# One order for five engines: an earlier bias chain, zeros for a waiting TensorE, a third operand set, one branch at the end

## The chip, the cores and the metric

The kernel runs on one core of one Trainium2 chip. The metric is the device time of one execution in microseconds (us). The engines are TensorE (PE for matmuls, PEld for its weight loads), VectorE (DVE), ScalarE (ACT), GpSimd (POOL) and SyncE (SP), which issues most DMAs.

## The reference

Three layers follow each other, all in float32 (the weights of the second layer are float64).

```python
# 1: causal attention with decay, q, k, v: (4, 8, 576, 64), f: (4, 8, 576)
scores = q @ k.T / sqrt(64)
cum = cumsum(log(clip(f, 1e-4, 1.0)), axis=-1)
scores = where(causal, -1e9, scores + cum[..., :, None] - cum[..., None, :])
attn = exp(scores - max(scores)); attn = attn / (sum(attn) + 1e-9)
x = (attn @ v), heads side by side        # (2304, 512)
# 2: dense layer with ELU, w_in (512, 2048), w_out (2048, 512)
h = x @ w_in; g = where(h > 0, h, exp(min(h, 0)) - 1); x = g @ w_out
# 3: eight experts, each token goes to one
logits = x @ w_gate + modality_bias[modality_id]; e = argmax(logits)
out = softmax(logits)[e] * (relu(x @ w1[e]) @ w2[e])
```

## The kernel before, in words

Every float32 product is made from two halves of an operand, a rounded one and its remainder, so TensorE multiplies two or three times for each product.

**Attention** (`attn`, `pair`) works on 16 pairs of heads, numbers 0 to 15. For a pair, SP loads q and k (`loads`, tiles `rq` and `rk` of pool `rqk`), TensorE transposes them (L572), ScalarE writes the rounded halves into `kb` and `qm` (L582), VectorE the remainders into `kx` and `qx` (L587), and SP copies the rounded halves beside the remainders (L593, L595). A first product `s1` (L617, with a causal mask from L620) gives the row maxima (VectorE, L635 and L637); these are transposed (L656) and written into row 96 of `qm` (L659). The second product `s2` (L670 and L673) then yields the scores transposed and already less their maximum, ScalarE takes the exponential (L692), GpSimd cuts the diagonal blocks (L697). The row sums come either from TensorE (pairs in `PE_SUM`) or from additions on GpSimd or VectorE (L705, chosen by `ADDPOOL`).

**The bias chain** (`attn_prep`) makes the decay term: SP loads f (L437), VectorE clips it (L443), ScalarE takes the logarithm (L446), VectorE adds it up along the row (L449), multiplies by -8 (L451), rounds (L452) and takes the remainder (L453). The two results, `nbr(0)` and `nbr(1)`, go to rows 64 and 65 of `kb`: for pair 0 by four small DMAs from SBUF (L559), for the other pairs by way of DRAM (L457, then L555). No `s1` can begin before its rows are there. `ms` fills the constant rows of `kb` and `qm` on GpSimd (L461 to L463).

The four tiles `kx`, `kb`, `qx`, `qm` are a *set*; there are two sets, and pair i takes whichever is free. Tile `xB` holds the attention's output for the second group of rows and is empty until the second batch element begins.

**Dense layer** (`convs`, `moe1`): in the first part, float64 weights are read as raw words and turned into two float32 halves in eight steps on ScalarE, VectorE and GpSimd (L849 to L879) and spilled to DRAM; `C7POOL` says whether the last step (L879) runs on VectorE or GpSimd for each of a weight block's two halves. The token rows go through in four steps (`STEPS`), each with eight groups of weights; the activation takes four operations `e1` to `e4` (L930 to L943), where `E4POOL` gives the last of a step to GpSimd. **Experts** (`route`, `tables`, `slot`): tokens are sorted into lists, `tables` makes the counts, and 2 + 9 slots of fixed size do the work; each slot ends in a scatter to the output (L1354). `rest` stands behind them: for either kind of slot it loads a count into a register of each engine (L1464) and jumps over further slots when there are none (L1465).

**The order** on all engines is written out ahead of time by a planner (`Sched`): each operation has a cost and a priority, and a simulated machine picks the lowest priority among those that could start. The table `SHIFT` moves the priorities of named groups of operations, so it decides the order on every queue, SP's included. Buffers come from named pools with a fixed number of slots.

Of the kernel before, what the change touches and what calls it, by code (L numbers as in the profile page):

```python
# [30 lines left out]
P = 128  # L31
# [169 lines left out]
class Kern:  # L201
# [71 lines left out]
    def pools(self):  # L273
# [14 lines left out]
        sc.pool("rqk", 2, tl(A, [96, 6, 2, D], F32, "rqk"))  # L288
# [16 lines left out]
    def consts(self):  # L305
# [4 lines left out]
        nc.vector.memset(self.ones64, 1.0)  # L310
        self.maskU = cp.tile([P, P], BF16, name="maskU")
# [112 lines left out]
    def attn_prep(self):  # L424
# [8 lines left out]
        def row(k):  # L433
            return sc[k][0:32, 0:S]
# [13 lines left out]
        def v2():  # L448
            nc.vector.tensor_tensor_scan(out=row(C), data0=row(O), data1=row(F), initial=0.0,  # L449
                                         op0=ALU.mult, op1=ALU.add)  # L450
            nc.vector.tensor_scalar(row(O), row(C), -8.0, None, op0=ALU.mult)  # L451
            nc.vector.tensor_copy(self.nbr(0), row(O))  # L452
            nc.vector.tensor_tensor(self.nbr(1), row(O), self.nbr(0).bitcast(F32), op=ALU.subtract)  # L453
# [17 lines left out]
        l = sc.op("SP", 0.45, l1, acq=[("pt", F)])  # L471
        n = sc.op("DVE", 0.6, one, acq=[("pt", O)])
        o = sc.op("DVE", 0.37, v1, [l])
        o = sc.op("ACT", 0.58, a1, [o])
        self.cumd = o = sc.op("DVE", 2.7, v2, [o, n], acq=[("pt", C)], rel=[C])
        self.nbd = o
        self.padd = sc.op("POOL", 0.6, pad, prio=0.5)
        self.nb8d = sc.op("SP", 0.9, l2, [o], rel=[O, F])
        self.sets, self.setd = [], []
        for s in range(2):  # L480
            st = {}
            for nm in ("kx", "kb", "qx", "qm"):
                st[nm] = ap.tile([P, 2, S], F32R, name=f"{nm}_{s}")
# [3 lines left out]
            sc.op("DVE", 0.18, lambda st=st: nc.vector.memset(st["ms"], 0.0), prio=-1.0)  # L487
            self.setd.append(sc.op("POOL", 2.6, lambda st=st: ms(st), prio=-1.0 + s))
            self.sets.append(st)

# [21 lines left out]
    def pair(self, i, t0, per, bg):  # L512
# [49 lines left out]
        got = op(None, 0.0, None, [], acq=[("set", st_)])  # L562
        ldb = [op("SP", 0.58 if i else 2.3, lb, [got, self.nbd if i == 0 else self.nb8d] + self.setd + self.first,
# [1001 lines left out]
```

## Time and profile before

| | |
|---|---|
| three timed runs | 924.23, 927.33, 928.87 us; median 927.33 |
| the profiled execution | 924.3 us, of which 922.4 us from the first to the last instruction |
| TensorE busy in the span | 860.8 us (93%), 5321 matmuls |
| VectorE, ScalarE, GpSimd busy | 704.1, 476.2, 284.2 us (76%, 52%, 31%) |
| moved by DMA | 174.39 MB, 189 GB/s |

The span's start is the zero of all times below. An engine counts as busy while it executes; branches, semaphore and register instructions and the issue of DMAs are not counted. Busy TensorE isn't TensorE at its best: matmuls overlap, and at the lower of its two clock levels the same work is busy for longer.

### The profile page before, as it was taken

Reading aid. Unit: us, or ns where it says so; the run is one execution under the profiler, and the core shown is the slowest. Engines: PE = TensorE matmul, PEld = TensorE weight load, DVE = VectorE, ACT = ScalarE, POOL = GpSimd, SP = SyncE. Lnnn points to the kernel's source line nnn. Section 1 sums busy time; section 2 is a strip of 40 time slices with the busy share of each in tenths; the row PEclk is TensorE's granted clock in tenths of the full one; section 3 lists DMA queues with packets and bytes.
Section 4 is the critical chain, followed back from the end, with each engine's and each line's share of the span. In section 5 each row is a group of like instructions: output and inputs, shape, how many; then the busy total and the mean of one; then the engine's idle time right before and its main releaser. Section 6 shows DMA issues by size and latency. Waiting matters only on the chain. (4 is left out here: it accounts for less than half of the span.)

```text
span 922.4 us, 15345 instructions
## 1 busy us (share of the span) xinstructions
PE 860.8 (93%) x5321; PEld 723.7 (78%) x5321; DVE 704.1 (76%) x1562; ACT 476.2 (52%) x923; POOL 284.2 (31%) x371
## 2 busy tenths in 40 slices
PE   4998998899999899999999999999999999999894
PEld 3776766676788788887777888898898888878783
DVE  6688799896899957769998569978797656677731
ACT  4676777676454464354463244346362545647520
POOL 4244467575101163024131010003013345344420
PEclk9999999999999999999999999999999999999998
DMA  6566788866963625458454525559154877688710
GB/s 138 146 189 197 213 224 225 241 241 229 286 254 107 156 82 140 157 150 218 131 183 151 182 92 183 188 215 390 73 152 152 273 235 238 237 267 283 255 62 28
DMA packets 111360, 174.39 MB, mean 189 GB/s; under 512 B 67150, under 2 KB 67168, under 8 KB 102695
## 3 DMA queue, kind: packets, MB, share of 16 engines
q1 hardware_dynamic: 108231, 163.54, 56.6%
q0 software_dynamic: 3040, 9.74, 2.8%
q8 instruction: 46, 0.75, 0.4%
q14 instruction: 43, 0.35, 0.1%
HBM read 136.87 MB, written 26.68 MB: 177 GB/s over the span
## 5 line engine op out<-in xcount | busy, mean ns | idle before, releaser
L926 PE MATMUL banks<-x_h,w_i 128*128 128x320 f32 (+1 forms) x768 | 208.1, 342 | 3.5 <-DVE ya L960 0.9
L953 PE MATMUL banks<-w_o,g_h 128*128 128x512 f32 x576 | 185.6, 403 | 4.9 <-DVE x_l L809 1.7
L926 PEld LDWEIGHTS banks<-x_h,w_i 128*128 128x128 f32 x768 | 135.8, 188 | 17.0 <-DVE ya L960 1.6
L697 POOL TENSOR_SCALAR_AFFINE_SELECT pt<-pt 128x128 f32<-128x128 f32 (+1 forms) x150 | 51.3, 356 | 276.2 <-ACT pt L692 274.4
L926 PE MATMUL banks<-x_l,w_i 128*128 128x320 f32 (+1 forms) x384 | 129.0, 336 | 0.0
L953 PEld LDWEIGHTS banks<-w_o,g_h 128*128 128x128 f32 x576 | 102.3, 190 | 26.3 <-DVE g_l L943 2.4
L953 PE MATMUL banks<-w_o,g_l 128*128 128x512 f32 x288 | 113.2, 393 | 0.0
L960 DVE TENSOR_TENSOR ya<-ya,banks 128x512 f32<-128x512 f32 x126 | 84.7, 681 | 24.5 <-PE banks L953 23.9
L930 ACT ACTIVATE e<-banks 128x320 f32<-128x320 f32 (+1 forms) x96 | 46.8, 488 | 89.2 <-PE banks L926 88.8
L692 ACT ACTIVATE pt<-banks 128x576 f32<-128x576 f32 (+4 forms) x160 | 60.4, 437 | 37.8 <-PE banks L673 32.3
L935 DVE SCALAR_TENSOR_TENSOR banks<-e,banks 128x320 f32<-128x320 f32 (+1 forms) x96 | 53.6, 558 | 32.1 <-ACT e L931 31.7
L1381 PE MATMUL banks<-xt_f_h,w_f 128*128 128x256 f32 x384 | 73.6, 286 | 3.8 <-DVE w_f L1312 1.8
L926 PEld LDWEIGHTS banks<-x_l,w_i 128*128 128x128 f32 x384 | 72.2, 188 | 4.9
L1056 DVE CUSTOM_DVE_ANT_0 junk<-ya,wgb 128x512 bf16<-128x512 f32 x104 | 71.4, 686 | 2.5 <-DMA wgb<-wgd 1.2
L1312 DVE TENSOR_TENSOR w_f<-wr_f,w_f 128x1024 fp32r<-128x1024 f32 x36 | 54.2, 1520 | 21.6 <-ACT w_f L1307 21.4
L1307 ACT ACTIVATE w_f<-wr_f 128x1024 fp32r<-128x1024 f32 x48 | 50.5, 1058 | 37.4 <-PE banks L1348 19.0
L1381 PEld LDWEIGHTS banks<-xt_f_h,w_f 128*128 128x128 f32 x384 | 61.5, 192 | 5.4 <-DVE w_f L1312 2.2
L939 ACT ACTIVATE g_h<-banks 128x320 fp32r<-128x320 f32 (+1 forms) x96 | 46.7, 487 | 36.2 <-DVE banks L935 35.6
L670 PE MATMUL banks<-qx,kx 128*128 128x288 f32 (+2 forms) x192 | 57.6, 316 | 7.8 <-ACT pt L692 2.3
L953 PEld LDWEIGHTS banks<-w_o,g_l 128*128 128x128 f32 x288 | 54.4, 189 | 12.2
L617 PE MATMUL banks<-kb,qm 96*128 96x288 f32 (+4 forms) x192 | 53.2, 366 | 11.2 <-DMA kb<-pt 5.7
L943 DVE TENSOR_TENSOR g_l<-banks,g_h 128x320 fp32r<-128x320 f32 (+1 forms) x96 | 52.7, 552 | 12.9 <-ACT g_h L939 12.4
(263 smaller groups left out, 1922.1 us busy)
## 6 DMA issues: line engine op xcount, KB each, us to landing
w_i<-wspi SPq DMA_DIRECT2D x24, 1024.0 KB
w_o<-wspo SPq DMA_DIRECT2D x24, 1024.0 KB
wr_f<-in_moe_w SPq DMA_DIRECT2D x48, 512.0 KB
wr_h<-in_moe_w SPq DMA_DIRECT2D x24, 512.0 KB
raw_o<-in_moe_w_out SPq DMA_DIRECT2D x16, 512.0 KB
raw_i<-in_moe_w_in SPq DMA_DIRECT2D x16, 512.0 KB
wspo<-w_o SPq DMA_DIRECT2D x8, 1024.0 KB
wspi<-w_i SPq DMA_DIRECT2D x8, 1024.0 KB
```

Source lines behind the costliest of these rows:

```text
L617: nc.tensor.matmul(ps[:, o:o + n], st["qm"][0:96, hh, q0:q0 + P], st["kb"][0:96, hh, c0:c0 + n], start=True, stop=not diag)
L670: nc.tensor.matmul(ps[:kn, o:o + n], st["kx"][:, hh, k0:k0 + kn], st["qx"][:, hh, c0:c0 + n], start=True, stop=False)
L692: nc.scalar.activation(d, src, AF.Exp, scale=0.125)
L697: nc.gpsimd.affine_select(out=pt[:kn, o:o + kn], in_=pt[:kn, o:o + kn], pattern=[[1, kn]], compare_op=ALU.is_ge, fill=0.0, base=0, channel ...
L926: nc.tensor.matmul(ph[:, :n], a, b[:, c, c0:c1], start=(c == 0 and k == 0), stop=(c == 3 and k == 2))
L935: nc.vector.scalar_tensor_tensor((e if E4POOL[s] else sc[hk])[:, :n], e[:, :n], -1.0, sc[hk][:, :n], op0=ALU.add, op1=ALU.max)
L943: eng.tensor_tensor(sc[gk][1][:, c0:c0 + n], sc[ek if E4POOL[s] else hk][:, :n], sc[gk][0][:, c0:c0 + n].bitcast(F32), op=ALU.subtract)
L953: nc.tensor.matmul(py, a[:, sl], b, start=(fc == 0 and k == 0), stop=(fc == 1 and k == 2))
L960: nc.vector.tensor_tensor(y, y, py, op=ALU.add)
L1056: nc.vector.tensor_tensor_reduce(out=self.junk, in0=sc[yk], in1=w, scale=1.0, scalar=0.0, op0=ALU.mult, op1=ALU.add, accum_out=V["dt"][:, ...
L1312: eng.tensor_tensor(w[:, :, 1, :], sc["wr", nm, m, u], w[:, :, 0, :].bitcast(F32), op=ALU.subtract)
L1381: nc.tensor.matmul(sc["ch", nm, f // 2][:, z * 256:(z + 1) * 256], a, b[:, c, :], start=(c == 0 and k == 0), stop=(c == 3 and k == 2))
```

## The change

- **Bias chain first.** The load of f gets the lowest priority of all; the bias operations hold their place (`lock=True`); the multiplication and rounding become one instruction, and the remainder another that reads the running sum directly. A one-element logarithm (`lg1`) stands at the start of ScalarE's program.
- **Zeros multiplied.** Twelve operations of four 128x128 by 128x256 bf16 products of zeros are put into TensorE's order near the start.
- **Constant rows.** `ms` is split in two: the ones of `qm` are written by VectorE for the first two sets (whole lower half, one instruction), the rows of `kb` by GpSimd in two instructions. An operation waits for the rows of its own set, no longer for those of both.
- **A third set**, laid over `xB`, serves pair 2. **Four buffers** instead of two for q and k.
- **One branch at the end.** `tables` also makes `left`, the largest surplus over the slots that always run; `rest` tests that once, and the two old tests stand inside.
- **Order made anew.** All of `SHIFT` and the planner's other numbers differ. With them go: `PE_SUM` from pairs 0 to 3 to pairs 0, 1, 3, 5; additions on VectorE for pairs 2, 8, 11, 13 and 15 (before: pair 15); the last conversion step wholly on GpSimd; `e4` of the dense layer's last step on GpSimd; two neighbours in the order of the expert slots exchanged.

```diff
-        sc.pool("rqk", 2, tl(A, [96, 6, 2, D], F32, "rqk"))
+        sc.pool("rqk", 4, tl(A, [96, 6, 2, D], F32, "rqk"))
...
+        self.zero = cp.tile([P, 256], BF16, name="zero")
+        nc.vector.memset(self.zero, 0.0)
+        self.lg1 = cp.tile([P, 1], F32, name="lg1")
+        nc.scalar.activation(self.lg1, self.ones64[:, 0:1], AF.Ln)
...
-            nc.vector.tensor_scalar(row(O), row(C), -8.0, None, op0=ALU.mult)
-            nc.vector.tensor_copy(self.nbr(0), row(O))
-            nc.vector.tensor_tensor(self.nbr(1), row(O), self.nbr(0).bitcast(F32), op=ALU.subtract)
+
+        def v3():
+            nc.vector.tensor_scalar(self.nbr(0), row(C), -8.0, None, op0=ALU.mult)
+
+        def v4():
+            nc.vector.scalar_tensor_tensor(self.nbr(1), row(C), -8.0, self.nbr(0).bitcast(F32), op0=ALU.mult, op1=ALU.subtract)
...
-        def ms(st):
-            for nm in ("kb", "qm"):
-                nc.gpsimd.memset(st[nm][64:128].bitcast(F32), 0.0)
-            nc.gpsimd.memset(st["qm"][64:66].bitcast(F32), 1.0)
-            nc.gpsimd.memset(st["kb"][96:97].bitcast(F32), 1.0)
+        def ms(st, z):
+            if z == 0:
+                (nc.vector if st["ones"] == "DVE" else nc.gpsimd).memset(st["qm"][64:128].bitcast(F32), 1.0)
+            else:
+                nc.gpsimd.memset(st["kb"][64:128].bitcast(F32), 0.0)
+                nc.gpsimd.memset(st["kb"][96:97].bitcast(F32), 1.0)
+
+        def warm(z):
+            for _ in range(4):
+                nc.tensor.matmul(sc["warm", 0][:, 0:256], self.zero[:, 0:P], self.zero, start=True, stop=True)
...
-        l = sc.op("SP", 0.45, l1, acq=[("pt", F)])
+        l = sc.op("SP", 0.62, l1, acq=[("pt", F)], prio=-400.0)
...
+        sc.grp = "warm"
+        a = sc.op(None, 0.0, None, acq=[("p", ("warm", 0))], prio=0.0)
+        for z in range(WARM):
+            sc.op("PE", 0.43, lambda z=z: warm(z), [a], rel=[("warm", 0)], prio=20.0 + 0.1 * z)
...
-        sc.op(None, 0.0, None, s2s_ + pe + aug, rel=[st_])
+        sc.op(None, 0.0, None, s2s_ + pe + aug, rel=[("xB", 2) if i == 2 else st_])
...
+            if k == "f":
+                more = sm([1], "more")
+                nc.vector.tensor_scalar(more, end[:, 7:8], float(-SF), 0.0, op0=ALU.add, op1=ALU.max)
+            else:
+                left = self.left = sm([1], "left", I32)
+                nc.vector.scalar_tensor_tensor(left, end[:, 7:8], float(-SH), more, op0=ALU.add, op1=ALU.max)
...
-        for k, n0, n in (("f", SF, NF), ("h", SH, NH)):
-            tot = nc.values_load(self.tot[k][0:1, 0:1], min_val=0, max_val=n)
-            with self.tc.If(tot > n0):
...
+        left = nc.values_load(self.left[0:1, 0:1], min_val=0, max_val=max(NF - SF, NH - SH))
+        with self.tc.If(left > 0):
+            for k, n0, n in (("f", SF, NF), ("h", SH, NH)):
+                tot = nc.values_load(self.tot[k][0:1, 0:1], min_val=0, max_val=n)
+                with self.tc.If(tot > n0):
...
-PE_SUM = [True, True, True, True, False, False, False, False, False, False, False, False, False, False, False, False]
+PE_SUM = [True, True, False, True, False, True, False, False, False, False, False, False, False, False, False, False]
...
-C7POOL = [False, True]
-E4POOL = [False, False, False, False]
-ADDPOOL = [True, False, False, True, True, True, True, True, True, True, True, True, True, True, True, False]
...
+C7POOL = [True, True]
+E4POOL = [False, False, False, True]
+ADDPOOL = [False, False, False, False, True, True, True, True, False, True, True, False, True, False, True, False]
...
+WARM = 12
```

## Rows read from the trace of the kernel before

**Rows 1.** Windows: stretch, its length, each engine's busy us, clock, DMA share, GB/s.

```profile
0.00:17.09 17.09, 4.80 (x24) 3.72 (x25) 11.56 (x17) 9.90 (x13) 10.47 (x21) 1.00 0.58 134
17.09:33.90 16.81, 15.88 (x67) 13.20 (x68) 10.26 (x16) 4.66 (x10) 1.52 (x5) 1.00 0.60 166
...
40.00:225.00 185.00, 169.56 (x1124) 131.60 (x1124) 163.22 (x283) 131.07 (x255) 102.19 (x142) 0.99 0.74 215
225.00:440.00 215.00, 208.02 (x1362) 176.16 (x1361) 171.34 (x419) 105.57 (x248) 53.72 (x109) 0.99 0.59 175
440.00:860.00 420.00, 409.13 (x2399) 351.64 (x2399) 323.31 (x805) 203.98 (x368) 103.01 (x84) 1.00 0.59 203
...
909.50:922.40 12.90, 0.00 (x0) 0.00 (x0) 0.75 (x1) 0.00 (x0) 0.98 (x1) 0.70 0.09 27
```

**Rows 2.** Timeline, first 18 us: start, duration, engine, line, operation [idle before <-releaser].

```profile
3.62 0.62 SPq L437 DMA_DIRECT2D pt<-in_f  x1
...
6.41 1.09 DVE L443 TENSOR_SCALAR pt<-pt 32x576 f32<-32x576 f32 x1 [4.24 <-DMA pt<-in_f]
6.63 1.28 ACT L446 ACT_TABLE_LOAD   x1
...
7.92 0.68 ACT L446 ACTIVATE pt<-pt 32x576 f32<-32x576 f32 x1
...
8.64 1.34 DVE L449 TENSOR_TENSOR_SCAN pt<-pt,pt 32x576 f32<-32x576 f32 x1
...
10.02 1.01 DVE L451 TENSOR_SCALAR pt<-pt 32x576 f32<-32x576 f32 x1
...
11.06 0.78 DVE L452 CAST pt<-pt 32x576 fp32r<-32x576 f32 x1
...
11.87 0.74 DVE L453 TENSOR_TENSOR pt<-pt,pt 32x576 fp32r<-32x576 f32 x1
...
14.70 2.48 SPq L559 DMA_DIRECT2D kb<-pt  x4
...
17.12 0.39 PE L617 MATMUL banks<-kb,qm 96*128 96x64 f32 x1 [4.81 <-DMA kb<-pt]
```

**Rows 3.** Timeline, TensorE's matmuls around 33 us and around 40 us.

```profile
33.02 0.44 PE L670 MATMUL banks<-qx,kx 128*128 128x288 f32 x1
...
33.26 0.44 PE L673 MATMUL banks<-qm,kb 128*128 128x288 f32 x1
...
40.18 0.29 PE L670 MATMUL banks<-qx,kx 128*128 128x288 f32 x1
...
40.31 0.29 PE L673 MATMUL banks<-qm,kb 128*128 128x288 f32 x1
```

**Rows 4.** Lines L1464, L1465, L1561: instruction, ns min/median/max, first to last start us.

```profile
L1464 POOLq TENSOR_LOAD <-toth x1: 305/305/305, 916.5 to 916.5; - x1
...
L1465 PEldq COMPARE_BRANCH  x2: 3651/4042/4432, 906.3 to 910.6; - x2
...
L1465 POOLq INC_SWDGE_SEM  x2: 917/932/948, 915.5 to 917.5; - x2
...
L1561 POOLq DRAIN  x3: 40/107/3168, 918.4 to 922.2; - x3
```

**Rows 5.** Lines L879, L865, L461 by themselves, same columns, whole span.

```profile
L879 DVE TENSOR_TENSOR w_i<-raw_i,w_i x8: 677/692/1371, 59.9 to 216.7; 128x512 fp32r<-128x512 f32 x8
L879 POOL TENSOR_TENSOR w_i<-raw_i,w_i x8: 1287/1306/1329, 70.7 to 221.3; 128x512 fp32r<-128x512 f32 x8
...
L865 DVE TENSOR_SCALAR raw_i<-raw_i x16: 386/428/1197, 57.2 to 218.8; 128x512 uint32<-128x512 uint32 x16
...
L461 POOL MEMSET kb<- x2: 1053/1056/1058, 1.8 to 6.1; 64x1152 f32 x2
```

**Rows 6.** Groups by shape: busy us, mean ns, idle before; VectorE 440 to 870, GpSimd overall.

```profile
L943 DVE TENSOR_TENSOR g_l<-banks,g_h 128x320 fp32r<-128x320 f32 x32 | 15.5, 486 | 2.3 <-ACT g_h L939 2.2
...
L705 POOL TENSOR_TENSOR acc<-acc,pt 128x320 f32<-128x320 f32 x22 | 20.9, 950 | 0.3
```

More of the change, by code (lines that the diff above doesn't have):

```diff
@@ L470, in attn_prep @@
         sc.prio, sc.grp = -1.0, "prep"
-        l = sc.op("SP", 0.45, l1, acq=[("pt", F)])
+        l = sc.op("SP", 0.62, l1, acq=[("pt", F)], prio=-400.0)
         n = sc.op("DVE", 0.6, one, acq=[("pt", O)])
[L473 to L480, printed above, removed]
+        o = sc.op("DVE", 0.37, v1, [l], lock=True)
+        o = sc.op("ACT", 0.68, a1, [o])
+        o = sc.op("DVE", 1.34, v2, [o, n], acq=[("pt", C)], lock=True)
+        n1 = sc.op("DVE", 0.37, v3, [o], lock=True)
+        n2 = sc.op("DVE", 0.69, v4, [n1], rel=[C], lock=True)
+        self.nbd = [n1, n2]
+        self.padd = sc.op("POOL", 1.0, pad, prio=0.5)
+        self.nb8d = sc.op("SP", 1.2, l2, [n1, n2], rel=[O, F])
+        self.sets, self.setd, self.gots = [], [], []
+        for s in range(3):
             st = {}
-            for nm in ("kx", "kb", "qx", "qm"):
-                st[nm] = ap.tile([P, 2, S], F32R, name=f"{nm}_{s}")
+            if s < 2:
+                for nm in ("kx", "kb", "qx", "qm"):
+                    st[nm] = ap.tile([P, 2, S], F32R, name=f"{nm}_{s}")
             st["ms"] = ap.tile([P, 260], F32, name=f"m_{s}")
@@ L486, in attn_prep, with third @@
             st["ma"] = ap.tile([P, 1], F32, name=f"ma_{s}")
-            sc.op("DVE", 0.18, lambda st=st: nc.vector.memset(st["ms"], 0.0), prio=-1.0)
-            self.setd.append(sc.op("POOL", 2.6, lambda st=st: ms(st), prio=-1.0 + s))
+            st["ones"] = "DVE" if s < 2 else "POOL"
+            def third(st=st):
+                for z, (a, b) in zip(sc["xB", 2], (("kx", "kb"), ("qx", "qm"))):
+                    v = z[:].rearrange("p c n -> p (c n)")
+                    st[a], st[b] = [v[:, S * 2 * i:S * 2 * i + 2 * S].rearrange("p (h s) -> p h s", h=2) for i in range(2)]
+            al = [sc.op(None, 0.0, third, acq=[("xB", ("xB", 2))], prio=0.0)] if s == 2 else []
+            sc.op("DVE", 0.18, lambda st=st: nc.vector.memset(st["ms"], 0.0), prio=-1.0 + 2 * s)
+            self.setd.append([sc.op(st["ones"], 1.1, lambda st=st: ms(st, 0), al, prio=-1.0 + 2 * s),
+                              sc.op("POOL", 2.1, lambda st=st: ms(st, 1), al, prio=-1.0 + 2 * s)])
             self.sets.append(st)
+        sc.grp = "warm"
+        a = sc.op(None, 0.0, None, acq=[("p", ("warm", 0))], prio=0.0)
+        for z in range(WARM):
+            sc.op("PE", 0.43, lambda z=z: warm(z), [a], rel=[("warm", 0)], prio=20.0 + 0.1 * z)
     def attn(self, b, t0, per):
@@ L561, in pair @@
         sc.prio, sc.grp = t0, f"a{i}t"
-        got = op(None, 0.0, None, [], acq=[("set", st_)])
-        ldb = [op("SP", 0.58 if i else 2.3, lb, [got, self.nbd if i == 0 else self.nb8d] + self.setd + self.first,
+        if i == 2:
+            sc.tiles[st_] = (None, 0, self.sets[2])
+        got = op(None, 0.0, None, self.gots, acq=[] if i == 2 else [("set", st_)])
+        if i < 2:
+            self.gots.append(got)
+        setd = self.setd[i] if i < 3 else []
+        ldb = [op("SP", 0.58 if i else 2.3, lb, [got] + (self.nbd if i == 0 else [self.nb8d]) + setd + self.first,
                   rel=() if i else [("pt", "f"), ("pt", "one")])]
@@ L602, in pair @@
                 v = (nm, hh, key)
-                his[nm, hh] = op("ACT", 0.14 + S / 1200, lambda v=v: hi(*v), [t] + self.setd)
+                his[nm, hh] = op("ACT", 0.14 + S / 1200, lambda v=v: hi(*v), [t])
                 los[nm, hh] = op("DVE", 0.07 + S / 960, lambda v=v: lo(*v), [his[nm, hh]], rel=[key])
@@ L609, in pair @@
             op("ACT", 1.3, lambda: nc.scalar.activation(sc[st_]["ma"][:, 0:1], self.ident[:, 0:1], AF.Exp),
-               list(his.values()) + self.setd, prio=t0 - 1.0)
+               list(his.values()), prio=t0 - 1.0)
         def s1(j, hh, c0, n, key, o):
```

36 lines of the change are left out of this document (18 added, 18 removed), and 85 rows, old and new, of the table SHIFT.

## The prediction

> **What bounds the kernel now.** I read the table of windows first, then the list of waits for TensorE's gaps, then the timeline at both ends, and last the groups of the operations that change engines.
>
> The windows [rows 1] show three different states. In the first 17.09 us TensorE works 4.80 us: it stands still for 12.3 us. From there to 909.5 us it is nearly full: 95% up to 440 us, 97% up to 860 us. In the last 12.9 us it does nothing. VectorE is the second engine: 88% from 40 to 225 us, 80% and 77% in the next two stretches. So TensorE's own work sets the time, and there are four places where time can be found: the empty start, the rate at which TensorE works, the empty end, and the gaps between, which from 40 to 860 us come to 15.4 + 7.0 + 10.9 = 33.3 us [rows 1].
>
> The timeline says what the start waits for [rows 2]. The first score product begins at 17.12 us, released by a DMA into `kb`: the bias rows. Follow these back. Their four DMAs are issued from 14.70 us; the remainder that they carry was ready at 12.61 us (11.87 + 0.74); the chain began at 6.41 us when f landed; and f was issued at 3.62 us, behind four loads of q and k.
>
> The rate shows in the spacing of equal products [rows 3]. At 33 us, products of 288 columns follow each other by 0.24 us, at 40 us by 0.13 us. 288 columns in 0.24 us is 1.2 GHz, the lower level; at 0.13 us the engine is near the upper level, 2.4 GHz. The clock column of the windows prints 1.00 for both and doesn't help here; the spacing decides. TensorE had been busy 15.88 of 16.81 us before the rise, first with short masked score products and at the very end with s2 products in an unbroken row; only behind these did it speed up. So all work from 17.09 to 33.9 us ran at the lower level.
>
> **The change part by part.**
>
> *Bias chain, three terms.* (1) f goes to the head of SP's queue. At f's own issue time, 0.62 us, the four loads in front cost 2.5 us: -2.5. The loads of q and k are later by one issue, 0.62 us; they wait for nothing else, and the score product needs the bias later than their transposes. (2) The chain took 6.2 us from landing to remainder [rows 2]. Multiplication (1.01) and rounding (0.78) become one instruction: -0.9. A table load of 1.28 us ended at 7.91, 0.4 us after the clipping did; the one-element logarithm moves it to the idle start of ScalarE: -0.4. Clipping took 1.09 us and multiplying 1.01 us, while the nearest single-source operation needs as little as 0.39 us for 512 columns [rows 5] but is stretched at other times; I count 0.4 us of that as saved, since GpSimd's fillings still run beside it. Together -1.7; the bounds are -0.8 (only the rounding goes) and -2.5. (3) Between the ready remainder and the first of the four row DMAs lie 2.1 us in which SP issues other things. In the new order these rows come first, but a load that is being issued (0.62 us) can stand in front, and four buffers allow more of them: -1.5, bounds 0 and -2.1. Sum -5.7, bounds -3.3 and -7.1: the first score product at 11.4 us.
>
> *Zeros.* 48 products of 256 columns are, by the spacing of the 288-column ones, 0.21 us each at the lower level and 0.12 at the upper: 10.2 or 5.5 us, some 8 if the level rises halfway. TensorE is idle for 11.4 - 4.8 = 6.6 us before the new first product, and its transposes shrink too if the level rises. So I cost them at nothing; without any rise they overrun by 3.6 us. What they may buy: the 15.88 us of work at the lower level, times 0.13/0.24, is 8.6 us, 7.3 less. VectorE can't follow wholly: it was busy 10.26 of that stretch, and the remainders of two pairs that it did while TensorE waited now fall into it. I take half, -3.6, bounds 0 and -7.3.
>
> *Constant rows, third set, four buffers.* GpSimd's four fillings for each set become two; VectorE gets one of 1.06 us [rows 5] for each of two sets. They can lie ahead of f's landing, where VectorE waits: it stood idle 5.5 of the first 17.09 us [rows 1], 4.24 of them just before the clipping [rows 2]. If that cover is gone, they cost 2.1 us, out of the half that I left to VectorE. The third set and the buffers let pair 2 begin without a released set; nothing is freed later for it, since `xB` is empty until the second batch element. Both are at nothing by themselves: they are what lets the rest move up.
>
> *End.* After the last scatter has landed, GpSimd counts its DMA semaphores up (0.95 us), loads the second count at 916.49 us, branches, counts up again (0.92 us) and reaches the final drain at 918.42 us [rows 4]. With one branch the stretch from 916.49 to 918.42 goes: -1.9. TensorE's 4.4 us behind a branch lies under the scatter's landing either way. Bounds: -0.9 (one counting only) and -2.9 (the drain of 3.17 us shrinks by another). The two new one-element instructions in `tables` lie while TensorE works off the early slots; even at the 0.74 us of the bias subtraction each they would be 1.5 us without that cover.
>
> *The order and the balance.* TensorE keeps its sums, four pairs of them. VectorE loses 16 conversion steps of about 0.69 us or more (-11) [rows 5] and 32 remainders of 0.49 us (-15.5) and gets the additions of four more pairs; GpSimd gets 16 x 1.31 = 21 us and 32 x 0.95 = 30 us [rows 5, 6], with room for both: 102 of 185 us and 103 of 420 [rows 1]. Many of the waits from 40 to 225 us in the list end on VectorE, so some of the 33.3 us of gaps can close; but every other operation is placed anew as well, and a gap closed here opens there. I take -2, bounds -6 and +6.
>
> **Sum.** -5.7 - 3.6 - 1.9 - 2 = -13.2 us. Against the profiled execution's own 924.3 us that is 911.1. The median of the runs shown is 927.33, 3.0 above it, so I forecast **914** (927.3 - 13.2 = 914.1). All lower ends together (-7.1 - 7.3 - 2.9 - 6 = -23.3) give 904.
>
> **The rivals.**
>
> *B: the lower level stays for the score products.* For it: in the row of before, 16 us of nearly full work didn't raise the level until the unbroken s2 products came, and the score products follow the zeros. Against: the zeros are an unbroken row, as those were. Then the clock term is lost: -5.7 - 1.9 - 2 = -9.6, 917.7; if the zeros too run wholly at the lower level, another 3.6, 921. The Trainium skill ("TensorE: Matmul & The Clock Gate", Part 1) says that the slow clock is the default, released by sustained activity and given back after idling; by that, an early row of zeros works only if nothing empty lies behind it. The rise in this trace agrees; a fall at the start isn't shown here.
>
> *C: GpSimd and VectorE stand in each other's way, slower than before.* The 32 remainders `e4` move from 0.49 to 0.95 us and lie between ScalarE and the second product. A VectorE operation that takes 0.39 us alone took up to 1.20 [rows 5]. If 0.46 us of each reaches TensorE, 14.7 us are lost and the gain is gone: that is where it decides. If a third of them also wait 0.34 us, half of a VectorE operation of 0.69, it is 0.57 each, 18 us: 932. Against: TensorE has other groups' products to do meanwhile. The Trainium skill ("SBUF — State Buffer", Who interferes with whom) has the two engines exclude each other for whole instructions over a shared pair of ports when VectorE reads two SBUF inputs; the stretched maxima agree with it.
>
> *D: the early start is given back.* The conversion stage moves 215 GB/s with the DMA engines 74% busy [rows 1]. If its weights pace the stage, 9.3 us of start vanish in it: -3.9, 923.4. Against: between 40 and 225 us no wait of TensorE ends on a DMA, and SP itself mostly waits for the other engines.
>
> **Chances.** Forecast 0.65 (909 to 919), B 0.15, D 0.11, C 0.08; 0.01 below. A measurement here can tell about 0.5% from no change, 4.6 us: faster means below 922.7. Forecast and B are faster, with a little of D: 0.82. D is mostly the same: 0.10. C is slower: 0.08. The range goes from all lower ends to just past B with overrun: 904 to 922; D and C, 0.19 together, lie outside.
>
> **What the profile after would show.** The load of f as SP's first DMA; the first score product near 11.4 us (right between 10 and 14); products of 288 columns 0.13 us apart already in the first s2, not 0.24; one counting of semaphores and some 11 us between the last matmul and the end. TensorE's idle time from 40 to 860 us of its old place should be 27 to 39 us. The prediction is wrong if the score product starts early but the state that before had at 40 us comes less than 6 us sooner, or if the dense layer's last step shows waits of TensorE for `g_l` on GpSimd.

## The result, and the profile of the changed kernel

| | before | after |
|---|---|---|
| median of nine timed runs each, same chip | 927.11 us | 918.47 us |
| ratio, 95% interval | | 0.9916 [0.9894, 0.9939] |
| the profiled execution | 924.3 us | 917.9 us |
| its span | 922.4 us | 916.0 us |

The change gains 7.8 us (5.7 to 9.8 by the interval); the forecast was 13.2. The total fell inside the range and on the right side, 4.5 us above the forecast of 914. The sum that led there did not come out: its two largest terms moved nothing at the mark that they were to move, the first exponential. Now and then an execution is about 1% slower although the program is the same; the ratios in this document leave such executions out, the medians don't, and a2_more_zeros below, whose profiled execution was one, is read for its first 35 us alone. Marks that both traces have (first or last instruction of a line) show where the time changes:

| mark | before | after | difference |
|---|---|---|---|
| first score product `s1` | 17.12 | 16.03 | -1.1 |
| first row maximum | 19.00 | 19.71 | +0.7 |
| first exponential | 30.81 | 31.60 | +0.8 |
| end of the 40th exponential | 81.04 | 82.33 | +1.3 |
| first product of the experts | 666.96 | 665.24 | -1.7 |
| end of the last matmul | 909.50 | 906.61 | -2.9 |
| end of the span | 922.43 | 916.04 | -6.4 |

So the start lost 0.8 us, the stretch between the first exponential and the last matmul gained 3.7, the end 3.5: together the 6.4 us between the two spans. These are two single executions; the nine timed runs of the changed kernel alone lie between 914.18 and 921.77 us. Now the same views of the changed kernel. First the windows (columns as in [rows 1], which they answer), then the two windows that cut the span at the first exponential and the last matmul.

```profile
0.00:17.09 17.09, 11.50 (x88) 9.41 (x88) 14.72 (x22) 10.70 (x17) 9.30 (x20) 0.91 0.68 155
17.09:33.90 16.81, 14.31 (x62) 11.74 (x62) 11.83 (x18) 5.07 (x10) 1.10 (x5) 0.50 0.93 219
...
40.00:225.00 185.00, 172.37 (x1141) 134.73 (x1138) 153.23 (x271) 131.37 (x254) 112.75 (x148) 0.97 0.70 211
225.00:440.00 215.00, 206.78 (x1373) 176.31 (x1373) 176.96 (x448) 106.88 (x251) 42.94 (x88) 1.00 0.58 177
440.00:860.00 420.00, 408.77 (x2378) 351.23 (x2375) 317.39 (x769) 202.87 (x364) 132.34 (x113) 1.00 0.59 201
```

```profile
0.00:31.60 31.60, 23.52 (x138) 18.94 (x139) 25.44 (x38) 13.78 (x21) 9.30 (x20) 0.72 0.80 186
31.60:906.60 875.00, 842.07 (x5232) 710.16 (x5231) 670.27 (x1513) 462.44 (x902) 301.91 (x365) 0.99 0.60 192
```

The row for 17.09 to 33.9 us says 0.50 in the clock column: the lower level, now in so many words. TensorE worked 11.50 of the first 17.09 us instead of 4.80, mostly on zeros, and is no further on for it. From 40 to 860 us it is idle for 12.6 + 8.2 + 11.2 = 32.1 us, before 33.3 [rows 1]. VectorE has 25.44 us of work up to the first exponential; cut at its own first exponential, before has 20.71.

The timeline of the first 20 us answers [rows 2].

```profile
0.82 0.40 SPq L441 DMA_DIRECT2D pt<-in_f  x1
...
3.99 1.02 DVE L468 MEMSET qm<- 64x1152 f32 x1 [0.28 <-issue]
...
5.04 0.84 DVE L447 TENSOR_SCALAR pt<-pt 32x576 f32<-32x576 f32 x1
...
8.01 1.29 DVE L457 TENSOR_SCALAR pt<-pt 32x576 fp32r<-32x576 f32 x1
...
9.36 1.80 DVE L621 TENSOR_TENSOR kx<-banks,kb 64x576 fp32r<-64x576 f32 x2
...
11.19 1.52 DVE L621 TENSOR_TENSOR qx<-banks,qm 64x576 fp32r<-64x576 f32 x2
...
12.75 0.75 DVE L460 SCALAR_TENSOR_TENSOR pt<-pt,pt 32x576 fp32r<-32x576 f32 x1
13.03 2.46 SPq L588 DMA_DIRECT2D kb<-pt  x4
...
15.10 1.22 PE L606 MATMUL banks<-ident,rq 96*128 96x96 f32 x6 [2.18 <-DVE xB_h L621]
...
16.03 0.40 PE L651 MATMUL banks<-kb,qm 96*128 96x64 f32 x1
...
19.73 0.53 PE L651 MATMUL banks<-kb,qm 96*128 96x192 f32 x1 [2.50 <-DVE qx L621]
```

f is SP's first DMA. But the clipping (L447) begins when the second filling with ones (L468) ends, at 5.04 us; the remainder (L460) has its input at 9.30 and begins at 12.75, behind pair 0's remainders; and the first score product stands behind the last transposes (L606). After it TensorE waits 2.50 us more, until VectorE has done the remainders of three pairs.

The spacing [rows 3] and the end [rows 4]: s2 products of 288 columns at 34 us, still 0.24 us apart; then the lines of the branch and of the final drain (columns as in [rows 4]).

```profile
33.82 0.44 PE L704 MATMUL banks<-qx,kx 128*128 128x288 f32 x1
34.06 0.44 PE L707 MATMUL banks<-qm,kb 128*128 128x288 f32 x1
```

```profile
L1505 PEldq COMPARE_BRANCH  x1: 3402/3402/3402, 903.4 to 903.4; - x1
...
L1505 POOLq INC_SWDGE_SEM  x1: 948/948/948, 911.1 to 911.1; - x1
...
L1606 POOLq DRAIN  x3: 40/107/3168, 912.0 to 915.8; - x3
```

One counting at 911.1 us, and the drain follows directly at 912.0. The remainders of the dense layer's last step, moved to GpSimd [rows 6], take 0.88 us each in the median, a little less than the 0.95 that was counted:

```profile
L977 POOL TENSOR_TENSOR g_l<-e,g_h x32: 866/880/1160, 547.0 to 652.6; 128x320 fp32r<-128x320 f32 x32
```

### The profile page after: what moved, and what is told of

It is laid out like the page before. It is cut to its first block, busy times and chain, and to the rows that moved or that the text cites. A ratio compares the mean times of both kernels' runs of the same rounds, so it can differ in the third digit from the quotient of the medians.

```text
span 916.0 us, 15468 instructions
## 1 busy us (share of the span) xinstructions
PE 865.6 (94%) x5369; PEld 729.1 (80%) x5369; DVE 696.5 (76%) x1551; ACT 476.2 (52%) x923; POOL 312.2 (34%) x386
## 5 line engine op out<-in xcount | busy, mean ns | idle before, releaser
L731 POOL TENSOR_SCALAR_AFFINE_SELECT pt<-pt 128x128 f32<-128x128 f32 (+1 forms) x150 | 53.5, 377 | 282.5 <-ACT pt L726 280.4
L1090 DVE CUSTOM_DVE_ANT_0 junk<-ya,wgb 128x512 bf16<-128x512 f32 x104 | 75.9, 730 | 1.3
L1352 DVE TENSOR_TENSOR w_f<-wr_f,w_f 128x1024 fp32r<-128x1024 f32 x36 | 51.4, 1442 | 31.0 <-ACT w_f L1347 30.9
L1347 ACT ACTIVATE w_f<-wr_f 128x1024 fp32r<-128x1024 f32 x48 | 50.4, 1058 | 40.0 <-DMA wr_f<-in_moe_w 14.8
L1388 PE MATMUL banks<-w_f,g_f_h 128*128 128x512 f32 x192 | 61.8, 403 | 0.8 <-DVE g_f_l L1429 0.8
L651 PE MATMUL banks<-kb,qm 96*128 96x64 f32 (+3 forms) x180 | 52.5, 379 | 7.5 <-DVE qx L621 2.5
L704 PE MATMUL banks<-qx,kx 128*128 128x288 f32 (+1 forms) x180 | 53.2, 314 | 4.7 <-DVE t L804 1.8
L977 POOL TENSOR_TENSOR g_l<-e,g_h 128x320 fp32r<-128x320 f32 x32 | 28.9, 907 | 79.4 <-ACT g_h L973 79.3
L1421 PE MATMUL banks<-xt_f_l,w_f 128*128 128x256 f32 x192 | 54.0, 281 | 0.0
```

The costliest lines, as they stand in the source:

```text
L651: nc.tensor.matmul(ps[:, o:o + n], st["qm"][0:96, hh, q0:q0 + P], st["kb"][0:96, hh, c0:c0 + n], start=True, stop=not diag)
L704: nc.tensor.matmul(ps[:kn, o:o + n], st["kx"][:, hh, k0:k0 + kn], st["qx"][:, hh, c0:c0 + n], start=True, stop=False)
L731: nc.gpsimd.affine_select(out=pt[:kn, o:o + kn], in_=pt[:kn, o:o + kn], pattern=[[1, kn]], compare_op=ALU.is_ge, fill=0.0, base=0, channel ...
L1090: nc.vector.tensor_tensor_reduce(out=self.junk, in0=sc[yk], in1=w, scale=1.0, scalar=0.0, op0=ALU.mult, op1=ALU.add, accum_out=V["dt"][:, ...
L1347: nc.scalar.activation(sc["w2", nm, m, u][:, :, 0, :], sc["wr", nm, m, u], AF.Copy)
L1352: eng.tensor_tensor(w[:, :, 1, :], sc["wr", nm, m, u], w[:, :, 0, :].bitcast(F32), op=ALU.subtract)
```

## The experiments

Three theories were on record first. **T1**: the new order spends the early start itself; the remainder of the bias stands behind five VectorE operations and the score products behind transposes whose banks VectorE frees late. **T2**: VectorE's own work bounds the time up to the first exponential, so neither clock nor bias matters. **T3**: a gain of the start is given back in the conversion stage (rival D).

Unless a diff says otherwise, a kernel below is the changed one: its planned order as a list, some operations moved in it, issued as it then stands (the program itself is edited in e5_two_tests and c2_old_tables). The diffs show that order; "..." marks lines left out. One table has all results; "first" is the first exponential, "last" the end of the last matmul, "tail" from there to the end of the span, in the profile.

| kernel | median us | ratio to before, 95% interval | first | last | tail |
|---|---|---|---|---|---|
| a0_same_order | 919.24 | 0.9906 [0.9873, 0.9940] | 30.86 | 907.36 | 9.98 |
| a1_score_first | 927.06 | 1.0002 [0.9973, 1.0031] | 39.32 | 918.33 | 9.85 |
| a2_more_zeros | 919.49 | 0.9909 [0.9879, 0.9939] | 30.05 | | |
| a3_no_zeros | 921.84 | 0.9962 [0.9932, 0.9992] | 31.20 | 908.91 | 9.83 |
| b1_pair2_late | 925.05 | 0.9995 [0.9968, 1.0021] | 36.55 | 913.55 | 9.76 |
| b2_pair2_late_bias | 922.83 | 0.9965 [0.9942, 0.9989] | 35.43 | 914.60 | 9.65 |
| e5_two_tests | 925.56 | 0.9982 [0.9952, 1.0013] | 31.61 | 909.08 | 12.30 |
| b4_before_f_first | 925.63 | 1.0007 [0.9981, 1.0033] | 30.59 | 911.10 | 12.66 |
| c1_old_engines | 915.28 | 0.9894 [0.9866, 0.9922] | 30.78 | 902.29 | 9.52 |
| c2_old_tables | 944.49 | 1.0197 [1.0159, 1.0236] | 31.56 | 932.50 | 9.61 |
| c3_chain | 918.07 | 0.9906 [0.9876, 0.9935] | 30.88 | 904.87 | 9.63 |
| c4_chain_zeros | 921.97 | 0.9948 [0.9923, 0.9973] | 32.57 | 912.35 | 9.76 |

**a0_same_order**: nothing moved.

> The changed kernel with its own order, issued from a recorded list; the yardstick for the others of this series. Every theory: 0.992 of the time before (0.989 to 0.994), first score product near 16.0 us, lower level from about 14 to 35 us.

0.9906 beside 0.9916 for the changed kernel itself: the way of issuing costs nothing. The two profiles of this one order differ by 0.7 us at the first exponential and 1.3 us in the span; that is the grain of a single trace at the start. Over the whole span it is coarser, as the timed runs show, so a difference of a few us between two traces counts only where other traces or the timing agree.

**a1_score_first**: T1's remedy.

```diff
 VectorE: v3 (rounded half of the bias)
+VectorE: v4 (remainder of the bias)
 VectorE: remainders of pair 0
-VectorE: v4
...
+SP: bias rows of pair 0
 SP: last load of pair 1, a load of v
-SP: bias rows of pair 0
...
-TensorE: transposes of pair 2, of pair 1
 TensorE: s1 of pair 0, with VectorE's maxima
+TensorE: transposes of pair 1, of pair 2
```

> The remainder of the bias directly behind its rounding on VectorE, the bias rows ahead of other loads on SP, and pair 0's score products and maxima ahead of the transposes of pairs 1 and 2; all else in the order of the changed kernel. Theory 1 (the new order spends the early start itself: the remainder stands behind five other VectorE operations and the score products behind transposes whose banks VectorE frees late; the stop lets the clock fall): first score product near 12 us instead of 16.0, no gap over 1 us on TensorE from there to 35 us, 4 to 8 us less than the changed kernel in all. Theory 2 (VectorE's work bounds the first 40 us): the score product comes early, the first exponential doesn't (31.6 us, at most 1 us sooner), 0 to 1 us less. Theory 3 (what the start gains is given back in the conversion stage): the state of 40 us comes 4 us sooner or more, the end less than 1 us.

The first score product came at 14.36 us, 1.7 sooner than in the changed kernel, and the first exponential at 39.32, 8.5 us later than in a0. TensorE's longest waits are ahead of the first product, inside the transposes and behind them:

```profile
14.36 0.27 PE L651 MATMUL banks<-kb,qm 96*128 96x64 f32 x1 [3.81 <-DMA kb<-pt]
...
23.96 1.22 PE L606 MATMUL banks<-ident,rq 96*128 96x96 f32 x6 [2.69 <-DVE m L669]
...
28.15 1.22 PE L606 MATMUL banks<-ident,rk 96*128 96x96 f32 x6 [2.97 <-DVE qx L621]
...
32.32 0.53 PE L651 MATMUL banks<-kb,qm 96*128 96x192 f32 x1 [1.51 <-DVE xB_h L621]
```

The transposes had filled a wait that was there anyway. The edit also puts pair 1's last load of q behind the bias rows, to 14.08 from 10.12 us, but the transposes of that q wait for VectorE's maxima and not for the load. T1's remedy is refuted. The 8.5 us arrive whole at the end: (1.0002 - 0.9906) x 927 = 8.9, 4 either way. That speaks against T3 and rival D: a late start isn't made up in the conversion stage. An early start that is given back, which is what both say, no run had.

**a2_more_zeros** and **a3_no_zeros**: the clock.

```diff
 TensorE: zeros, transposes of pair 0, zeros
+TensorE: 8 x zeros, 224 columns
 TensorE: transposes of pair 2
+TensorE: 20 x zeros
 TensorE: transposes of pair 1
+TensorE: 26 x zeros
 TensorE: s1 of pair 0
```

```diff
-TensorE: 12 x 4 products of zeros
```

> The changed kernel's order with 54 more products of zeros (224 columns each) in three places where its TensorE stands still between 10 and 20 us; no other operation moves. Theory 1: the level stays at the upper one from about 4 us on, the products from 20 to 35 us run at 0.13 us for 288 columns, first exponential near 26 us instead of 31.6, 3 to 7 us less in all. Theory 2: the level stays up but VectorE's maxima set the pace, first exponential at most 1 us sooner, 0 to 1 us less. Theory 3: the first exponential 3 us sooner or more, the end less than 1 us.

> The changed kernel's order without any product of zeros. Theory 1: the zeros raise the level only for the transposes, and it has fallen before the first score product; without them 0 to 1 us more. The prediction's own clock term would be 3.6 us more. Theory 2: no difference.

The windows of a2_more_zeros over the time after the first zeros, and those of the changed kernel:

```profile
14.10:18.10 4.00, 2.35 (x22) 1.80 (x20) 2.63 (x5) 3.00 (x5) 0.00 (x0) 1.00 0.30 64
18.10:21.60 3.50, 3.50 (x21) 2.88 (x20) 3.13 (x5) 0.88 (x2) 0.00 (x0) 0.51 0.63 136
21.60:34.60 13.00, 12.63 (x95) 10.52 (x94) 10.22 (x16) 6.40 (x16) 2.70 (x10) 1.00 1.05 246
```

```profile
4.00:14.10 10.10, 7.00 (x66) 5.77 (x64) 9.43 (x12) 6.71 (x11) 6.11 (x10) 1.00 0.97 220
14.10:34.60 20.50, 16.74 (x72) 14.07 (x73) 14.75 (x22) 7.64 (x15) 1.33 (x5) 0.50 0.80 187
```

In the changed kernel the zeros do raise the level, from 4 to 14.1 us, but only transposes and zeros are there to profit: it falls in the 2.2 us of waiting ahead of 15.10, just before the score products. (In a0_same_order and c1_old_engines, with the same wait, it falls 1.0 and 0.8 us behind its end; that the wait makes it fall is argued from its place.) With 54 products more it is lower for 3.5 us only, and the score products run at the upper level: from the first maximum to the first exponential they take 30.05 - 21.02 = 9.0 us instead of 31.60 - 19.71 = 11.9. So the clock is worth 2.9 us there, against T2. But the zeros themselves pushed the first maximum from 19.71 to 21.02, and the time is that of a0. Without any zeros the first maximum comes at 20.38 and the time is 0.0056 x 927 = 5 us above a0 (1 to 9); where they come from beyond 0.7 us at the first maximum (0.3 at the first exponential), the trace doesn't show.

**b1_pair2_late** and **b2_pair2_late_bias**: T2's remedy, alone and with the early bias.

```diff
-pair 2: transposes, halves, remainders ahead of s1 of pair 0
 pair 0: s1 and maxima
+pair 2: transposes, halves, remainders
 pair 1: s1 (rest) and maxima
```

```diff
 VectorE: v3
+VectorE: v4
 VectorE: remainders of pair 0
-VectorE: v4
...
 SP: loads of pair 1
+SP: bias rows of pair 0
 SP: a load of v
-SP: bias rows of pair 0
```

> The changed kernel with one edit of its order: the transposes, rounded halves and remainders of pair 2 come behind pair 0's last row maximum. T2 (VectorE's work bounds the time up to the first exponential): 3.05 us of pair 2's remainders leave VectorE's queue ahead of pair 0's maxima, so the first exponential comes at 28.0 to 29.5 us and not at 30.9 to 31.6, and the end 2 to 3 us sooner than in the changed kernel: 915 to 917 beside about 918.5. Rival (pair 2's transposes fill a wait that is there anyway): the first exponential at 31 us or later, the wait of TensorE near 15 us grows by what the transposes took, some 2 us, and the time is 918 to 921.

> The same edit, and the remainder of the bias right behind its rounded half on VectorE (at about 9 us and not 12.75), its four row DMAs on SP behind pair 1's last load. If the late remainder is what kept the first score product at 16 us, it begins at 12 to 13 us now, and with VectorE relieved the first exponential comes at 25.5 to 28 us: 913 to 916. By T2 alone the early bias adds nothing to the edit before: first exponential 28.0 to 29.5, the same time within 1.5 us. By the rival (the bias operations push the remainders that the transposes wait for) it is later than without: above 31 us, 919 to 925.

Both missed: first exponential at 36.55 and 35.43. The timeline of b1_pair2_late from 14 us on says why:

```profile
14.80 1.19 PE L606 MATMUL banks<-ident,rq 96*128 96x96 f32 x6 [3.12 <-DMA rq<-in_q]
...
17.38 1.53 DVE L621 TENSOR_TENSOR qx<-banks,qm 64x576 fp32r<-64x576 f32 x2 [2.32 <-ACT qm L616]
...
30.55 0.63 PE L651 MATMUL banks<-kb,qm 96*128 96x320 f32 x1 [3.55 <-DVE xB_l L621]
```

With pair 2 out of the way VectorE stood idle for 2.32 us, because pair 1's transposes waited 3.12 us for pair 1's own load of q, which landed at 14.8. T2 in its simple form falls: a load holds the start as well. And in their new place pair 2's transposes hold banks that pair 1's score products need (3.55 us). These two delays, 5.7 and 4.6 us against a0, again reach the end, whole as far as the timing tells (0.0089 and 0.0059, 8.2 and 5.5 us, each with about 4 either way).

**e5_two_tests**: the end alone undone.

```diff
-left = nc.values_load(self.left[0:1, 0:1], ...)
-with self.tc.If(left > 0):
-    for k, n0, n in (("f", SF, NF), ("h", SH, NH)):
+for k, n0, n in (("f", SF, NF), ("h", SH, NH)):
         tot = nc.values_load(self.tot[k][0:1, 0:1], ...)
         with self.tc.If(tot > n0):
```

> The changed kernel with the end of the kernel before: the two counts loaded and tested one behind the other, at the outermost level. If the branch is worth what the trace of before showed between the second load and the drain, the time is 1.9 to 2.0 us above the changed kernel and the stretch from the last matmul to the end of the span 11.4 us in place of 9.4. If the whole difference of the two stretches (12.9 against 9.4) is the branch's: 3.5 us. If most of the difference is how long the last scatter takes to land: under 1 us.

The lines of the branch in its profile:

```profile
L1507 PEldq COMPARE_BRANCH  x2: 3371/3752/4132, 905.9 to 909.9; - x2
...
L1507 POOLq INC_SWDGE_SEM  x2: 917/932/948, 914.4 to 916.4; - x2
```

Two countings again, 2.0 us apart, and a tail of 12.30 us. The ten other profiles with one branch have 9.43 to 9.98, the two of the old order 12.93 and 12.66: the branch is worth 2.3 to 3.5 us. Of that 2.0 is the second load and counting. Another 1.0 lies ahead of the first counting: from its start to its landing the last scatter takes 3.0 to 3.1 us in the ten traces with one branch and 4.0 to 4.2 in the three with two (this one and the two of the old order). Why it lands later there is open; what is left of the spread is when the scatter starts. The timing says 7 us with an interval of about 4 on either side: it agrees with the upper values of the trace and isn't sharper.

**b4_before_f_first**: the kernel before, with one edit.

```diff
+SP: load of f
 SP: loads of pair 0
-SP: load of f
```

> The kernel before with one edit: the load of f at the head of SP's queue. The forecast counted 2.5 us for this step alone: first score product at 14.6 and not 17.1 us, first exponential up to 2.5 us sooner than 30.8, time 924.5 beside 927. T2: VectorE stood idle for 4.24 us ahead of the clipping here and fills that now, but the same work stands between the score products and the first exponential: the score product comes 2 to 2.5 us sooner, the first exponential 0 to 1 us, and the time changes by 0 to 1 us.

The timeline of its start:

```profile
2.83 1.33 DVE L443 TENSOR_SCALAR pt<-pt 32x576 f32<-32x576 f32 x1 [0.66 <-DMA pt<-in_f]
...
6.77 0.65 ACT L582 ACTIVATE kb<-banks 64x576 fp32r<-64x576 f32 x1 [4.66 <-PE banks L572]
7.44 1.28 ACT L446 ACT_TABLE_LOAD   x1
...
8.73 0.68 ACT L446 ACTIVATE pt<-pt 32x576 f32<-32x576 f32 x1
...
15.45 2.48 SPq L559 DMA_DIRECT2D kb<-pt  x4
...
17.87 0.39 PE L617 MATMUL banks<-kb,qm 96*128 96x64 f32 x1 [4.75 <-DMA kb<-pt]
```

The clipping begins 3.6 us sooner, and the first score product 0.75 us later. The logarithm stands in ScalarE's queue behind pair 0's first rounded half, which waits for a transpose, which waits for a load that is now 0.5 us later. In the old order the forecast's -2.5 for this step doesn't come: it was the distance on one queue, and the chain runs through four. (The changed kernel has the logarithm first on ScalarE, at 5.92 us and not 7.92; there the time is lost further on, see below.)

**c3_chain** and **c4_chain_zeros**: the bias chain freed of the delays that [rows 2] of after had shown, then 38 products of zeros added in the three places of a2_more_zeros.

```diff
 VectorE: ones of qm, first set
+VectorE: clip
 VectorE: ones of qm, second set
-VectorE: clip
 VectorE: scan, v3
+VectorE: v4
 VectorE: remainders of pair 0
-VectorE: v4
...
 SP: loads of pair 1
+SP: bias rows of pair 0
 SP: a load of v
-SP: bias rows of pair 0
```

> The changed kernel with the bias chain unblocked: the clipping ahead of the second filling with ones on VectorE, the remainder right behind the rounded half, the row DMAs behind pair 1's loads. The two delays that the trace of the changed kernel shows (clipping 2.2 us behind the landed f, remainder 3.4 us behind its input) go; the remainder should be ready at 7 to 8 us and not 13.5. If the chain bounds the first score product, that begins at 11 to 13 us. If the transposes ahead of it bound it, through VectorE's remainders, it begins at 14.5 to 15.5, the first exponential comes 0.5 to 1.5 us sooner (30 to 31), and the time is within 1.5 us of the changed kernel's.

> The same chain and 38 more products of zeros, 224 columns each, in the waits ahead of the first score product, fewer than in the run that added 54. If from the first full row of score products TensorE's rate bounds the start (10.5 us of them at the lower level in the changed kernel), the level stays up but for a few us, the first exponential comes at 27.5 to 29 and the time is 2 to 3 us below the changed kernel: ratio to before 0.987 to 0.990. If VectorE bounds it anyway, 30 us and 0.990 to 0.992.

The timeline of c3_chain:

```profile
8.34 0.75 DVE L460 SCALAR_TENSOR_TENSOR pt<-pt,pt 32x576 fp32r<-32x576 f32 x1
...
10.11 0.84 SPq L562 DMA_DIRECT2D rq<-in_q  x1
...
11.05 3.35 SPq L588 DMA_DIRECT2D kb<-pt  x4
...
14.48 1.19 PE L606 MATMUL banks<-ident,rq 96*128 96x96 f32 x6 [2.06 <-DMA rq<-in_q]
...
15.38 0.40 PE L651 MATMUL banks<-kb,qm 96*128 96x64 f32 x1
...
15.69 0.39 PE L651 MATMUL banks<-kb,qm 96*128 96x64 f32 x1
...
19.01 0.53 PE L651 MATMUL banks<-kb,qm 96*128 96x192 f32 x1 [2.85 <-DVE qx L621]
```

The remainder was ready at 9.1 us, 4.4 sooner, and the first score product came 0.65 us sooner; the first exponential stayed at 30.88 (30.86 in a0) and the ratio at 0.9906. The bias no longer comes last. What does is in the row at 14.48: pair 1's transposes, which stand ahead of the score products, wait for the last load of q, issued at 10.11. But the bias is only just out of the way. The 4.4 us end in SP's queue, which comes to the four row DMAs at 11.05, behind that load; the fourth, issued at 13.83, lands at 15.56 (in the changed kernel at 16.63), 0.1 us before the second score product at 15.69. Earlier transposes alone would have met that next. The extra zeros came at the wrong time: the level held until 18.4 us, fell for the whole row of score products (to 35.4), and the first maximum moved from 18.99 to 20.67. The 1.7 us are in the first exponential (32.57) and in the time (0.0042, 3.9 us, nearly as much either way).

**c1_old_engines**: the order kept, 48 operations back on VectorE.

```diff
-eng = nc.gpsimd if C7POOL[u] else nc.vector
+eng = nc.gpsimd if u else nc.vector
...
-eng = nc.gpsimd if E4POOL[s] else nc.vector
+eng = nc.vector
```

> The changed kernel in its own order, but the 16 conversion steps and the 32 remainders of the dense layer's last step stand on VectorE again, each at the same place in the order. The forecast counted the balance with the order as -2 us. If the lighter VectorE is where the gain of the middle comes from, 26 us of work return to it and the time is 2 to 6 us above the changed kernel (ratio to before 0.993 to 0.998). If the moved operations were hidden on either engine, the time is the same within 1 us (ratio near 0.991). If rival C holds in part (the remainders on GpSimd come late to the second product), the last step is faster than in the changed kernel and the ratio is below 0.990.

0.9894 against 0.9906 and 0.9916, with intervals that overlap widely: moving this work to GpSimd gained nothing and cost at most a little. This is the fastest kernel measured here, but can't be told from the changed one.

**c2_old_tables**: all parts of the change, planned with the tables of the kernel before.

```diff
-SHIFT, PE_SUM, PAIR, C7POOL, E4POOL, ADDPOOL, XPOOL, DUR, ORDER, ... of the changed kernel
+the same names with the values of the kernel before
```

> All parts of the change (f first, zeros, third set, four buffers, fewer constant rows, one branch) with the planner's tables of the kernel before: shifts, engines of the moved operations, sums, slot order. If the parts make the gain, only the end and the start are there: 922 to 925 by the branch's 2.5 to 3 us alone. If the gain of the middle comes from the order made anew, nothing of it is here. A rival: the old table doesn't fit the new parts, so that the order it gives is worse than that of the kernel before, and the time is above 927.

18 us slower than before: the rival came true, the old tables don't fit the new parts. Two of its windows, and the first of them in the kernel before:

```profile
85.00:225.00 140.00, 127.59 (x728) 98.66 (x725) 116.91 (x192) 95.50 (x176) 71.35 (x90) 0.94 0.70 214
225.00:440.00 215.00, 203.33 (x1333) 172.46 (x1332) 158.36 (x376) 101.82 (x239) 52.03 (x102) 0.98 0.54 168
```

```profile
85.00:225.00 140.00, 128.60 (x767) 100.06 (x764) 124.08 (x198) 100.81 (x187) 83.88 (x101) 0.99 0.75 225
```

In the first TensorE is busy for about as long as before, but at a granted clock of 0.94 and not 0.99, and for 728 products in place of 767 (830 in the changed kernel); in the second it is busy for 4.7 us less than before [rows 1]. The start is less than a microsecond worse (31.56); from the end of the 40th exponential to the dense layer's last product it takes 607.3 us, before 589.2. The loss is in the middle, where this kernel has the parts and not the order.

## Why the prediction was right, and where it was wrong

**Bias chain, -5.7: failed.** The step that failed is "the first score product at 11.4 us"; it came at 16.03 (15.60 in a0_same_order), and the first exponential 0.8 us later than before (in a0 at the same time as before). Three things were wrong in it. *The fillings "at nothing"*: VectorE's cover for them was the wait for f, 4.24 us [rows 2], and the same edit removed that wait. f is there by 2.83 us where the trace has an idle VectorE (b4_before_f_first), so the fillings cost 2.2 us of the chain. *The remainder*: I counted its instruction and not its place in the queue, another 3.45 us. Subtracting the two gives 10.4 for the product; c3_chain, without them, has it at 15.38. *The premise*: nothing comes of the bias alone, since it was only one of several chains that end near each other, and part of its wait only moves to SP's queue. (The term's third part, -1.5 for rows that come first on SP, came in the changed kernel only because the remainder was late: the issue begins at 13.03, ahead of the remainder's end at 13.50. With the remainder ready at 9.1 the rows wait 2.0 us for SP again.) Before, the bias rows released the product at 17.12 and VectorE finished the remainders of two pairs at 18.07.

**Third set and four buffers "at nothing by themselves": failed.** They let pair 2 in, and it comes ahead of pair 1. In SP's queue pair 2's loads stand at 4.06 to 6.72 us, pair 1's at 6.85 to 11.08. Between 3 and 14.5 us the packets of this queue fill 93.6% of the 16 DMA engines; before, the same stretch has 74.6%, and pair 1's transposes start at 9.88 and go on at 11.09 without a wait.

```profile
DMA packets 7627, 2.45 MB, mean 213 GB/s; under 512 B 7499, under 2 KB 7499, under 8 KB 7627
...
q1 hardware_dynamic: 7627, 2.45, 93.6%
```

On VectorE the remainders of a third pair, 3.05 us, stand ahead of the second row of score products. Both delays are shown; that pair 1's load is late because of pair 2's is argued from the queue and the share. A kernel that loads pair 1 first and transposes pair 2 behind pair 1's score products wasn't tried, so whether the start can be had that way is open.

**Clock, -3.6: the size was near, the event didn't happen.** Rival B came: the level fell at 14.1 us and the score products ran at 0.50. What it would have been worth at the first exponential is 2.9 us (a2_more_zeros). The prediction had the condition in its own text on B, that nothing empty may lie behind the zeros, and its sum went by the unbroken row alone: a wait follows them. The Trainium skill ("TensorE: Matmul & The Clock Gate", Part 1) has the slow clock return after idling; a fall in that wait, or within 1.0 us of it, agrees in kind. One thing stays open: without the zeros the timing is 5 us longer (1 to 9), and only 0.3 us of that is there at the first exponential.

**End, -1.9: right in kind, too small.** 3.5 us between the two traces, 2.3 to 3.5 over all, around the bound of 2.9. The second load and counting are the 1.9 that were forecast; the 1.0 us by which the last scatter lands sooner was missing.

**Order and balance, -2: right for the wrong half.** The stretch from the first exponential to the last matmul is 875.0 us instead of 878.7. The same order takes 876.5 and 877.5 in a0_same_order and e5_two_tests, the old order 880.5 in b4_before_f_first, so the gain is 1.2 to 5.5 us. TensorE works 842.07 us of it (window above), and stands idle for 32.9. The same window of before:

```profile
30.81:909.50 878.69, 843.17 (x5244) 709.73 (x5243) 682.66 (x1531) 463.79 (x906) 272.74 (x349) 0.99 0.60 192
```

It has 35.5 us of idle time. Over the five traces the new order has 31.2 to 32.9 and the old 35.5 and 38.6, so closed gaps account for most of the gain. The lighter VectorE, which the forecast named as the reason, isn't it (c1_old_engines, 29.3 us of idle time); what is left is the order, which the parts also need not to lose 18 us (c2_old_tables). That it is the order is argued by what is left over; which of its moves closes the gaps wasn't separated.

**Rival C** didn't come: in the list of TensorE's waits from 440 to 860 us all that end on `g_l` name VectorE, 1.0 us together. Of the stretched operations that the prediction calls in agreement there, only L879 reads two inputs; L865 reads one [rows 5]. **Rival D** had no early start to give back; the four kernels with a later start, which isn't made up, speak against it.

**The signs that the prediction named.** f as the first DMA, one counting, a tail near 11 us (9.4) and 27 to 39 us of idle time (32.1) came; the score product between 10 and 14 us didn't, nor 0.13 us between the first s2 products in this profile (in a0_same_order, where the level rises again at 29.8 us, they have it). Neither sign of being wrong came, though two terms failed: the first supposes an early score product, and the second, a wait for `g_l` on GpSimd, has nothing to do with the start.

So the total was inside the range because the end and the middle gave 3.3 us more than their terms, which made up a third of the 9.3 us that bias and clock did not give. That is luck: no rival had bias and clock fail together, and the other two terms alone give 927.3 - 3.9 = 923.4, outside the range. That 918.47 lies next to rival B's 917.7 is luck as well, since B keeps the whole bias term.

## What to carry to other kernels

A transfer that is issued earlier moves the end of its chain only if every in-order queue on the way has the next step in front: follow it through each of them, and ask which other chain ends within a microsecond or two of the one removed. Cover that an edit relies on ("VectorE waits there") has to be taken from the kernel after the edit, since the edit itself may remove the wait. Work that keeps a clock level up has to end where the real work begins: in a wait behind it the level was lost again here, and put into the path it held the real work up, so neither run with more zeros was faster than the kernel that it started from.

## What the runs showed of the hardware

- The level fell in the wait of 2.2 us ahead of 15.10 us, after 10 us at the upper level, and in two other profiles up to 1.0 us behind that wait. In the new order, where the start isn't later, it falls again at 60 to 63 us, in a wait of 1.9 to 2.9 us for banks that ScalarE holds or up to 1.3 us behind it, and stays down for 6.8 us in the changed kernel's profile and 13.7 in that of a0_same_order; before, the wait at the same place was 1.33 us and the level stayed. It costs less than it looks: from the first to the 40th exponential 50.7 us in both, before 50.2.
- The last scatter landed 3.0 to 3.1 us after its start in the ten traces with one branch behind it and 4.0 to 4.2 in the three with two; the reason is open.
- f, 72 KB, was in use 2.0 us after its issue on an empty queue (0.83 to 2.83), and 2.8 us behind four loads (3.62 to 6.41, [rows 2]).
- The loads of q and k are made of small packets: 7499 of the 7627 between 3 and 14.5 us are under 512 B. There 93.6% busy engines move 213 GB/s, 228 at full share; between 85 and 225 us of the changed kernel, where larger ones are among them (31.48 MB in 22732 packets, 16056 of them small), 72% move 225 GB/s, 312 at full share. The Trainium skill ("DMA: Bandwidth & Descriptors", Specifications) asks for transfers of at least 512 B for the full rate; these two rates agree.
